# Attention and four experts on one core: where the last expert's first layer and its weight sums stand

## The chip, the cores and the metric

The kernel runs on one core of a Trainium2 chip. The metric is the device time of one execution in microseconds. A core has five engines, each with its own queue of instructions in order: TensorE (PE in the profile; PEld is its weight load), VectorE (DVE), ScalarE (ACT), GpSimd (POOL) and SyncE (SP, which here only issues DMAs). They wait for each other through semaphores. "Clock" is the TensorE clock that the throttle granted, as a share of full speed.

## The reference

Attention over 4 batches, 8 heads, 768 positions and head size 64; three heads see everything before them, five see 4 sink positions and a window of 64. Its output, as 3072 tokens of 512, goes through four experts that are summed with the tokens' weights.

```python
# attention
scores = scale * np.matmul(q, k.transpose(0, 1, 3, 2))
mask = np.where(retr[0, :, 0, 0, None, None], full_mask, stream_mask)
...
attn = np.matmul(a, v)                      # a: softmax of the masked scores
# experts: N, D = 3072, 512; E = 4, F = 1024
x = np.ascontiguousarray(attn_out.transpose(0, 2, 1, 3)).reshape(B * S, H * D)
p = domain_probs / (domain_probs.sum(-1, keepdims=True) + 1e-09)
for e in range(E):
    h = np.maximum(x @ w1[e], 0.0)
    out += p[:, e:e + 1] * (h @ w2[e])
```

## The kernel before

All matrices are held in f16. The 3072 tokens are 24 tiles of 128. The work has two strands. `attention(b, c)` makes the attention of half a batch (384 tokens, three tiles). `moe_steps()` makes the experts: tiles 0 to 2 together, then tile 3 alone ("the single tile"), both by `plain_steps`, and then ten pairs of tiles, 4-5 to 22-23, by `pair_steps`. Both strands are Python generators that yield after each step with the TensorE time that the step will take. The loop at the end of the kernel writes out the steps of the experts and, whenever the sum of the yielded times (weighted with a share) has passed a plan, the next step of attention. Instructions go into each engine's queue in this order, so the order of the whole program is fixed by hand. `require(g)` makes sure that an attention half is written out before something reads it.

**The single tile.** For each expert e: eight first-layer outputs (L983) with a Relu on ScalarE (L996), two half second layers (L1004) and an update of the output on VectorE (L1016, L1020). Behind experts 0 to 2 `last_weight_sum(e)` makes one VectorE subtraction for the second layer (L939, a helper, `minus`, that records all subtractions). Behind expert 1 the first pair's input for expert 0 is scaled. Behind expert 3 stand the four `first_weight_sums()`: the weights' sums and differences for expert 3's first layer, 128x1024 each. The fourth is made in place, in expert 3's own weights.

**A pair, first layer.** A token's weight is put on its input before the first layer (`scale_inputs`, L1066; the Relu lets a positive factor through). The inputs of experts 0 and 2 share one place in the buffer `xs`, expert 1 has its own, and expert 3 (EW) a third, with two more places for sums. Experts 0, 1 and 2 are plain: `plain_layer1(e)` has four steps of eight 256-column matmuls (L1100), each with one Relu (L1109). Expert 3 is done by a seven-product scheme of Strassen and Winograd (`winograd_layer1`): seven products of eight 128-column matmuls (L1152) in two PSUM buffers, x and y, with sums of its inputs before (`scaled_sums`: three small VectorE operations), copies of results (`keep`, ScalarE, L1162) and additions (`add`, VectorE, L1168 and L1174) between them. `keep(0)` writes a buffer "s1", `keep(1)` and `keep(2)` write "o1", which has the same memory (tag "o", one buffer) as the output tile `o` of the second layer. A product that goes on in the bank of an earlier one has to wait for the copy or the addition that reads it.

**A pair, second layer.** All four experts are one product of 4096 by 512, again in seven products (L1234), each in two halves, with sums of weights (`tsb`) and of activations (L939, L1074), copies (L1252, L1302) and additions (`add`, L1255). Behind the fifth product the next pair's input for expert 0 is scaled. Behind the sixth the first half of the output is stored, behind the seventh the second half (L1262, SP).

**Order in a pair's first layer.** `scale_inputs(nt0, 1)` comes first. The list `sums` is worked off, one entry behind each plain step. `load_probs(nxt)`, which loads the next pair's token weights through SP, stands ahead of expert 2.

**Queues around it.** SP issues the stores, the token weights and, for attention, the DMA transposes of keys, queries and results (L255, L718). GpSimd issues the loads of q, k and v. VectorE also masks attention's exponentials (L666), scales its results (L705 to L712, L779) and copies keys by windows and rows (L282, L286, L290, L266). ScalarE makes the exponentials (L662) and logarithms (L774, L784). The four "pA" banks are shared by plain steps and attention's scores.

Of the kernel before, what the change touches and what calls it, by code (L numbers as in the profile page):

```python
# [12 lines left out]
ALU = mybir.AluOpType  # L13
# [4 lines left out]
def kernel(  # L18
# [33 lines left out]
    nc = tc.nc  # L52
    P = 128
    B, H, S, D = q.shape
    E, DM, F = moe_w1.shape
# [43 lines left out]
    def bank():  # L99
        return pA.tile([P, 512], FP32, name="pA", bufs=4)  # L100
# [5 lines left out]
    HT = F // P // 2  # L106
# [4 lines left out]
    EW = E - 1  # L111
    KH, FN = DMP // 2, F // 2
# [19 lines left out]
    XS = 3 * DMP * 2 * P  # L132
# [247 lines left out]
    for h in range(H):  # L380
        if h == 2:
            nc.sync.dma_start(
                out=v_s32, in_=v[0, :, 0:NS, :].rearrange("h r d -> r h d")
# [16 lines left out]
        out=probs, in_=moe_domain_probs.rearrange("(t p) e -> p t e", p=P)  # L400
# [121 lines left out]
    def mm_ns(cols):  # L522
        return cols / 2.4 + 2.5
# [407 lines left out]
    def b_rows(k, n, e):  # L931
        f0 = e * FTP + k * HT
        return w2sb[:, f0 : f0 + HT, n * HN : (n + 1) * HN]
# [4 lines left out]
    def minus(out, a, b):  # L938
        nc.vector.tensor_tensor(out=out, in0=a, in1=b, op=ALU.subtract)  # L939
# [7 lines left out]
    def w1_part(j, k):  # L947
        return w1sb[:, EW * DMP + j * KH : EW * DMP + (j + 1) * KH, k * FN : (k + 1) * FN]

    def first_weight_sums():  # L950

        t = [t1sb[:, n, :, :] for n in range(3)]
        return [
            lambda: minus(t[0], w1_part(0, 1), w1_part(0, 0)),
            lambda: minus(t[1], w1_part(1, 1), t[0]),
            lambda: minus(t[2], w1_part(1, 0), t[1]),
            lambda: minus(w1_part(0, 1), w1_part(1, 1), w1_part(0, 1)),
        ]

    def last_weight_sum(e):  # L960

        minus(b_rows(0, 1, e), b_rows(1, 1, e), b_rows(0, 1, e))
# [68 lines left out]
    def pieces(nt0):  # L1031

        g0, j0 = divmod(nt0, 3)
        n0 = min(3 - j0, PT)
        yield g0, j0 * P, 0, n0
        if n0 < PT:
            yield g0 + 1, 0, n0, PT - n0

    pB_of = {}
    xs_of = [None]  # L1040

    def load_probs(nt0):
        pB_of[nt0] = moe.tile([P, PT, E, P], FP32, name="pB", tag="pB", bufs=1)
        rows = p_rows[nt0 : nt0 + PT, :]
        nc.sync.dma_start(
            out=pB_of[nt0].rearrange("p t e x -> p (t e x)"),
            in_=bass.AP(rows.tensor, rows.offset, [[0, P], [1, PT * E * P]]),
        )

    def scaled(e):  # L1050
        n = 2 if e == EW else e % 2
        x = xs_of[0][:, n * DMP * PC : (n + 1) * DMP * PC]
        return x.rearrange("p (c x) -> p c x", c=DMP)

    def scale_inputs(nt0, e):

        if xs_of[0] is None:
            xs_of[0] = moe.tile([P, XS + 2 * KH * P], FP16, name="xs", tag="xs", bufs=1)
        xs = scaled(e)
        for g, c0, t0, n in pieces(nt0):  # L1060
            require(g)
            xin = xT[g][:, :, c0 : c0 + n * P].rearrange("p c (t x) -> p c t x", t=n)
            o = xs[:, :, t0 * P : (t0 + n) * P].rearrange("p c (t x) -> p c t x", t=n)
            pb = pB_of[nt0][:, t0 : t0 + n, e, :]
            pb = pb.rearrange("p t (c x) -> p c t x", c=1)
            nc.vector.tensor_tensor(  # L1066
                out=o, in0=xin, in1=pb.to_broadcast([P, DMP, n, P]), op=ALU.mult
            )

    def input_sums(k0, k1):  # L1070
        k = slice(k0, k1)

        def s1():
            nc.vector.tensor_tensor(  # L1074
                out=S1[:, k, :], in0=A21[:, k, :], in1=A22[:, k, :], op=ALU.add
            )

        return [
            s1,
            lambda: minus(S3[:, k, :], A11[:, k, :], A21[:, k, :]),  # L1080
        ]
# [4 lines left out]
    def pair_steps(nt0, nxt):  # L1086

        sums = []

        def step_done():  # L1090
            if sums:
                sums.pop(0)()

        def plain_layer1(e):
            xs = scaled(e)
            for f0 in range(0, FTP, 2):
                ps = bank()
                for f in range(2):
                    for ct in range(DMP):
                        nc.tensor.matmul(  # L1100
                            out=ps[:, f * PC : (f + 1) * PC],
                            lhsT=w1sb[:, e * DMP + ct, (f0 + f) * P : (f0 + f + 1) * P],
                            rhs=xs[:, ct, :],
                            start=(ct == 0),
                            stop=(ct == DMP - 1),
                        )
                b0 = 2 * (f0 // HT)
                k0 = e * HT + f0 % HT
                nc.scalar.activation(  # L1109
                    out=blocks[:, b0 : b0 + 2, k0 : k0 + 2, :].rearrange(  # L1110
                        "p t f x -> p f t x"
                    ),
                    in_=ps.rearrange("p (f t x) -> p f t x", f=2, t=2),
                    func=AF.Relu,
                )
                step_done()
                yield 2 * DMP * mm_ns(PC), 0.5

        def x_part(i, j):
            return scaled(EW)[:, j * KH : (j + 1) * KH, i * P : (i + 1) * P]  # L1120

        def x_sum(n):
            x = xs_of[0][:, XS + n * KH * P : XS + (n + 1) * KH * P]
            return x.rearrange("p (c x) -> p c x", c=KH)

        def scaled_sums():
            def s1():
                nc.vector.tensor_tensor(
                    out=x_sum(0), in0=x_part(1, 0), in1=x_part(1, 1), op=ALU.add
                )  # L1130

            return [
                s1,
                lambda: minus(x_sum(1), x_sum(0), x_part(0, 0)),
                lambda: minus(x_part(1, 0), x_part(0, 0), x_part(1, 0)),
            ]

        def winograd_layer1():

# [64 lines left out]
            yield ns, 0.5  # L1204

        scale_inputs(nt0, 1)
        sums += [lambda: scale_inputs(nt0, EW)]
        if nt0 == pair0:
            sums += [lambda: last_weight_sum(E - 1)]
        sums += scaled_sums()  # L1210
        yield from plain_layer1(0)
        products = winograd_layer1()
        for e in (1, 2):
            if e == 1:
                scale_inputs(nt0, 2)
            elif nxt is not None:
                load_probs(nxt)
            for step in plain_layer1(e):
                yield step
                step = next(products, None)  # L1220
                if step is not None:
                    yield step
            sums += input_sums(0, 2 * HT) if e == 1 else input_sums(2 * HT, 4 * HT)
        for op in sums:
            op()

# [2 lines left out]
        x = pO.tile([P, DM], FP32, name="pO", bufs=2)[:, 0:HN]  # L1229
# [24 lines left out]
        def add(n, ps, i, j):  # L1254
            nc.vector.tensor_tensor(  # L1255
                out=o[:, i, j * HN : (j + 1) * HN], in0=ps, in1=s[:, n, :], op=ALU.add
            )

        def store(i, j=None):
            r = slice((nt0 + i) * P, (nt0 + i + 1) * P)  # L1260
            c = slice(0, DM) if j is None else slice(j * HN, (j + 1) * HN)
            nc.sync.dma_start(out=out[r, c], in_=o[:, i, c])  # L1262
# [31 lines left out]
        yield half  # L1294
        yield from product(y, S4, b(1, 1), False)
        add(1, y, 0, 1)
        store(0)
        if last:
            store(1, 1)
        yield half  # L1300
        yield from product(x, A22, t(2), False)
        nc.scalar.copy(out=o[:, 1, 0:HN], in_=x)  # L1302
        if last:
            store(1, 0)
        else:
            store(1)
        yield half

    pairs = list(range(pair0, NTILE, PT))

    def moe_steps():
        for e in range(E):
            if e == 1:
                turn_probs()
            yield from plain_steps(0, 3, e, lambda: xT[0], (e % 2) * FTP * CH)
            weight_sums(e)
        for e in range(E):
            n0 = (e % 2) * FTP * P
            yield from plain_steps(3, 1, e, lambda: xT[1][:, :, 0:P], n0)
            if e + 1 < E:  # L1320
                last_weight_sum(e)
            if e == E - 3:
                scale_inputs(pairs[0], 0)
        for op in first_weight_sums():
            op()
        for n, nt0 in enumerate(pairs):
            yield from pair_steps(nt0, pairs[n + 1] if n + 1 < len(pairs) else None)

# [55 lines left out]
    def require(a):  # L1384
        drained = False
        while state["a"] <= a:
            attention_step()
            drained = True
        if drained:
            tick(LAG)  # L1390
        while any(g <= a for _, _, g in behind):
            behind.pop(0)[1]()
# [48 lines left out]
```

The softmax here doesn't subtract the row's maximum and nothing guards it: scores larger than these inputs give would overflow.

## Time and profile before

| what | us |
|---|---|
| median of 5 runs | 386.87 (385.84 to 388.4) |
| the profiled execution, time | 386.8 |
| its span | 384.9 |
| TensorE busy | 373.2 (97%) |
| VectorE busy | 268.7 (70%) |
| ScalarE busy | 229.3 (60%) |
| GpSimd busy | 111.2 (29%) |
| mean granted clock of TensorE | 0.996 |

The shares are averages over stretches with different loads: up to about 90 us the kernel starts up, loads weights and works on tiles 0 to 3 beside attention. Then come the ten pairs, at 90.9, 125.9, 156.8, 185.4, 215.4, 244.4, 272.5, 302.7, 329.8 and 355.8 us (the first step's start of each), with attention beside the first eight. The last pair's second layer begins at 369.4 and TensorE ends before 382. In the timeline a row gives start, duration, engine, line, operation, output and input; in brackets stands the idle time of the engine before it and what ended it. Merged rows ("x2") give the time of all of them.

### The profile page before, as it was taken

What the parts mean: (1) busy time and instruction counts of PE and PEld (TensorE: products, weight loads), DVE (VectorE), ACT (ScalarE), POOL (GpSimd) and SP (SyncE); (2) the same over time, 40 slices, a digit from 0 to 9 for tenths busy, and PEclk for the clock granted to TensorE, in tenths of its full rate; (3) what the DMA queues carried; (4) which work ended last, traced back from release to release, by engine and by line L of the source; (5) the groups of instructions that cost most, each with busy time, mean ns of one, the idle gap of its engine ahead of it and who ended that gap; (6) DMA issues with size and microseconds to landing.
All of it is one profiled execution on the core that took longest, in us unless ns stands there. A gap on an engine that the chain in (4) does not pass through costs nothing.

```text
span 384.9 us, 9934 instructions
## 1 busy us (share of the span) xinstructions
PE 373.2 (97%) x4054; PEld 313.2 (81%) x4054; DVE 268.7 (70%) x590; ACT 229.3 (60%) x476; POOL 111.2 (29%) x152
## 2 busy tenths in 40 slices
PE   8999899998899999999999999999999999999996
PEld 4755456576798898899998988899998999998995
DVE  7746687567886878877766757977767867665460
ACT  3863568647486777665674775665665675450630
POOL 8933662953037217403710116403200000000000
PEclk9999999999899999999999999999999999999999
DMA  9999999999389989963990489964700210200001
GB/s 160 165 209 200 184 190 184 146 190 121 53 131 85 134 134 86 160 133 26 140 105 14 98 131 60 161 133 29 110 35 12 71 54 2 95 19 27 29 2 54
DMA packets 127193, 39.20 MB, mean 102 GB/s; under 512 B 116232, under 2 KB 120876, under 8 KB 127148
## 3 DMA queue, kind: packets, MB, share of 16 engines
q0 software_dynamic: 86816, 19.01, 56.5%
q1 hardware_dynamic: 38732, 19.18, 21.9%
q8 instruction: 31, 0.51, 0.5%
q10 hardware_dynamic: 1600, 0.39, 0.5%
q14 instruction: 14, 0.11, 0.1%
HBM read 44.88 MB, written 6.34 MB: 133 GB/s over the span
## 4 chain that ended last, share of the span: by engine, by line
PE 76%; DMA 11%; DVE 4%; POOL 4%; SPq 2%; ACT 2%; issue 1%; POOLq 0%; ACTq 0%
PE pO L1234 32%; PE pA L1100 24%; PE pO L1152 7%; DMA w2sb<-in_moe_w_dram 7%; PE pA L644 4%; PE pO L1004 2%; PE pA L983 2%; DMA qT<-q 2%; PE pV L692 2%; SPq L255 2%; PE pV L756 2%; DMA vR<-in_v_dram 1%; POOL vS L302 1%; DMA out_dram<-o 1%; POOL vR L296 1%
## 5 line engine op out<-in xcount | busy, mean ns | idle before, releaser
L1100 PE MATMUL pA<-xs,w1sb 128*128 128x256 f16 x960 | 120.9, 274 | 3.0 <-DVE xs L1066 3.0
L1234 PEld LDWEIGHTS <-hA 128*128 128x128 f16 x1120 | 106.5, 98 | 13.3 <-issue 0.5
L1100 PEld LDWEIGHTS <-w1sb 128*128 128x128 f16 x960 | 90.2, 98 | 13.2 <-DVE xs L1066 3.6
L1109 ACT ACTIVATE hA<-pA 128x512 f16<-128x512 f32 x120 | 71.1, 597 | 42.0 <-PE pA L1100 39.9
L662 ACT ACTIVATE es<-pA 128x384 f16<-128x384 f32 (+2 forms) x122 | 59.1, 511 | 32.7 <-PE pA L644 28.5
L1234 PE MATMUL pO<-w2sb,hA 128*128 128x256 f16 x640 | 78.1, 272 | 0.4 <-DVE hA L1168 0.4
L298 POOL DMA_DIRECT2D vS<-in_v_dram x30 | 29.6, 989 | 128.6 <-PE pV L756 121.2
L1234 PE MATMUL pO<-tsb,hA 128*128 128x256 f16 x480 | 58.9, 272 | 0.0
L1066 DVE TENSOR_TENSOR xs<-xT,pB 128x1024 f16<-128x1024 f16 (+1 forms) x52 | 48.7, 970 | 4.2 <-PE pA L1100 4.2
L939 DVE TENSOR_TENSOR hA<-hA 128x1024 f16<-128x1024 f16 x60 | 39.6, 685 | 0.6
L996 ACT ACTIVATE hA<-pA 128x384 f16<-128x384 f32 (+1 forms) x64 | 22.3, 386 | 20.3 <-PE pA L983 17.8
L983 PE MATMUL pA<-xT,w1sb 128*128 128x384 f16 (+1 forms) x256 | 31.7, 273 | 0.1
L1004 PE MATMUL pO<-w2sb,hA 128*128 128x512 f16 x128 | 30.5, 379 | 0.8 <-DMA w2sb<-in_moe_w_dram 0.8
L779 DVE TENSOR_TENSOR xT<-pV,rc 64x384 f16<-64x384 f32 x37 | 20.5, 555 | 11.8 <-ACT rc L784 9.6
L774 ACT ACTIVATE rc<-pV,eps 64x384 f32<-64x384 f32 x37 | 21.3, 575 | 9.1 <-PE pV L756 8.5
L983 PEld LDWEIGHTS <-w1sb 128*128 128x128 f16 x256 | 19.3, 98 | 8.4 <-issue 0.5
L666 DVE TENSOR_TENSOR es<-es,mS 128x384 f16<-128x384 f16 (+1 forms) x40 | 13.6, 345 | 16.8 <-ACT es L662 16.6
L1152 PE MATMUL pO<-xs,w1sb 128*128 128x128 f16 x320 | 25.1, 223 | 0.0
L644 PE MATMUL pA<-qT,kR 128*128 128x384 f16 (+2 forms) x120 | 22.9, 278 | 0.6 <-ACT qT L555 0.4
L1255 DVE TENSOR_TENSOR o<-pO,s 128x256 f32<-128x256 f32 x30 | 12.7, 422 | 14.9 <-PE pO L1234 11.8
L1074 DVE TENSOR_TENSOR hA<-hA 128x1024 f16<-128x1024 f16 x20 | 13.8, 688 | 12.7 <-ACT hA L1109 12.5
L1004 PEld LDWEIGHTS <-hA 128*128 128x128 f16 x128 | 11.9, 98 | 12.8 <-issue 1.0
(130 smaller groups left out, 468.8 us busy)
## 6 DMA issues: line engine op xcount, KB each, us to landing
pB<-p_rows SPq DMA_DIRECT2D x10, 512.0 KB, 3.4
out_dram<-o SPq DMA_DIRECT2D x19, 256.0 KB, 4.3
w1sb<-in_moe_w_dram POOLq DMA_DIRECT2D x8, 512.0 KB, 9.9
w2sb<-in_moe_w_dram POOLq DMA_DIRECT2D x4, 1024.0 KB, 13.2
vS<-in_v_dram POOLq DMA_DIRECT2D x30, 112.0 KB, 3.5
k_rows<-in_k_dram POOLq DMA_DIRECT2D x18, 128.0 KB, 4.2
q<-in_q_dram POOLq DMA_DIRECT2D x18, 128.0 KB, 5.5
vR<-in_v_dram POOLq DMA_DIRECT2D x24, 48.0 KB, 5.1
```

What stands on the lines that cost most here:

```text
L298: gp.dma_start(out=t[:, :, own_v(h)], in_=windows_of(v, b, h, c))
L644: nc.tensor.matmul(out=ps[:, o : o + nq], lhsT=key_tile(b, c, h, t), rhs=qTs[b, c][:, hp, q0 : q0 + nq], start=(n == 0 or not first), stop ...
L662: nc.scalar.activation(out=es[:, 0:cols], in_=ps[:, 0:cols], func=AF.Exp, scale=SC)
L939: nc.vector.tensor_tensor(out=out, in0=a, in1=b, op=ALU.subtract)
L983: nc.tensor.matmul(out=pss[ft][:, 0:cols_n], lhsT=w1sb[:, e * DMP + ct, ft * P : (ft + 1) * P], rhs=x[:, ct, :], start=(n == 0), stop=(n = ...
L996: nc.scalar.activation(out=hs[:, ft, :], in_=ps[:, 0:cols_n], func=AF.Relu)
L1004: nc.tensor.matmul(out=ps_o, lhsT=hs[:, ft, j * P : (j + 1) * P], rhs=w2sb[:, e * FTP + ft, :], start=(ft == 0), stop=(ft == FTP - 1),)
L1066: nc.vector.tensor_tensor(out=o, in0=xin, in1=pb.to_broadcast([P, DMP, n, P]), op=ALU.mult)
L1100: nc.tensor.matmul(out=ps[:, f * PC : (f + 1) * PC], lhsT=w1sb[:, e * DMP + ct, (f0 + f) * P : (f0 + f + 1) * P], rhs=xs[:, ct, :], start= ...
L1109: nc.scalar.activation(out=blocks[:, b0 : b0 + 2, k0 : k0 + 2, :].rearrange("p t f x -> p f t x"), in_=ps.rearrange("p (f t x) -> p f t x" ...
L1152: nc.tensor.matmul(out=ps[:, f * P : (f + 1) * P], lhsT=w[:, ct, f * P : (f + 1) * P], rhs=a[:, ct, :], start=(first and f == 0 and ct == ...
L1234: nc.tensor.matmul(out=ps, lhsT=a[:, k, :], rhs=b(k), start=(first and k == 0), stop=(k == KT - 1), skip_group_check=not first,)
```

## The change

The three small functions `x_part`, `x_sum` and `scaled_sums` leave `pair_steps` and stand beside it, and `scaled_sums` now does its three operations at once. Three of the four first-layer weight sums are made behind the single tile's experts 0, 1 and 2; the fourth goes to the first step of the first pair. The first pair's inputs for experts 0 and 3 are scaled behind experts 1 and 2 of the single tile, and its input sums are made behind expert 3. In the other pairs, expert 3's input is scaled behind the sixth product of the second layer of the pair before, and its sums are made behind the seventh. In the first layer the seven products follow the third plain step of expert 0 and each of the next six steps, up to the first step of expert 2; before, they followed the four steps of expert 1 and the first three of expert 2.

```diff
+    def scaled_sums():
+        nc.vector.tensor_tensor(
+            out=x_sum(0), in0=x_part(1, 0), in1=x_part(1, 1), op=ALU.add
+        )
+        minus(x_sum(1), x_sum(0), x_part(0, 0))
+        minus(x_part(1, 0), x_part(0, 0), x_part(1, 0))
...
         scale_inputs(nt0, 1)
-        sums += [lambda: scale_inputs(nt0, EW)]
         if nt0 == pair0:
-            sums += [lambda: last_weight_sum(E - 1)]
-        sums += scaled_sums()
-        yield from plain_layer1(0)
+            sums += [first_weight_sums()[3], lambda: last_weight_sum(E - 1)]
         products = winograd_layer1()
-        for e in (1, 2):
+        n = 0
+        for e in range(E - 1):
             if e == 1:
                 scale_inputs(nt0, 2)
-            elif nxt is not None:
+            elif e == 2 and nxt is not None:
                 load_probs(nxt)
             for step in plain_layer1(e):
                 yield step
-                step = next(products, None)
+                step = next(products, None) if n > 1 else None
+                n += 1
                 if step is not None:
                     yield step
-            sums += input_sums(0, 2 * HT) if e == 1 else input_sums(2 * HT, 4 * HT)
+            if e:
+                sums += input_sums(0, 2 * HT) if e == 1 else input_sums(2 * HT, 4 * HT)
...
         yield from product(y, S4, b(1, 1), False)
         add(1, y, 0, 1)
+        if nxt is not None:
+            scale_inputs(nxt, EW)
         store(0)
...
         yield from product(x, A22, t(2), False)
         nc.scalar.copy(out=o[:, 1, 0:HN], in_=x)
+        if nxt is not None:
+            scaled_sums()
...
             if e + 1 < E:
                 last_weight_sum(e)
-            if e == E - 3:
-                scale_inputs(pairs[0], 0)
-        for op in first_weight_sums():
-            op()
+            if e + 1 < E:
+                first_weight_sums()[e]()
+            if e > 0:
+                (
+                    lambda: scale_inputs(pairs[0], 0),
+                    lambda: scale_inputs(pairs[0], EW),
+                    scaled_sums,
+                )[e - 1]()
```

## The prediction

> **What bounds the kernel now.** I read the page first (parts 1 and 2), then who waited for whom on TensorE, then the timeline where a wait stands, then busy time in short stretches. TensorE is busy 97% of the span, and in the last pair, which has no attention beside it, the chain runs without a hole. So only two things can move the end: waits of TensorE, and its clock. The list of its waits:
>
> ```profile
> PE pA L1100 <- DVE xs L1066: 3.0, 2, 2.8
> PE pO L417 <- DVE early L402: 1.3, 1, 1.3
> ...
> PE pO L1234 <- DVE hA L1168: 0.4, 1, 0.4
> ```
>
> One wait of 2.8 us for a scaled input stands out. The timeline puts it at the start of the first pair (rows of VectorE and TensorE; a row in brackets ends with the idle time before it):
>
> ```profile
> 93.86 0.69 DVE L939 TENSOR_TENSOR t1sb<-w1sb 128x1024 f16<-128x1024 f16 x1
> 94.58 1.42 DVE L939 TENSOR_TENSOR t1sb<-w1sb,t1sb 128x1024 f16<-128x1024 f16 x2
> 95.91 0.69 DVE L939 TENSOR_TENSOR w1sb<-w1sb 128x1024 f16<-128x1024 f16 x1
> 96.51 2.35 DVE L1066 TENSOR_TENSOR xs<-xT,pB 128x1024 f16<-128x1024 f16 x2
> 97.78 1.05 PE L1100 MATMUL pA<-xs,w1sb 128*128 128x256 f16 x8 [2.76 <-DVE xs L1066]
> ```
>
> VectorE does the four first-layer weight sums and only then scales the input of expert 1, for which TensorE has been waiting since 95.02. There is a second cost behind it, seen in the stretches (length, busy PE, PEld, DVE, ACT, POOL, then granted clock):
>
> ```profile
> 17.14:20.55 3.41, 2.08 (x26) 1.59 (x24) 1.80 (x5) 2.01 (x5) 1.85 (x5) 1.00 1.40 194
> 95.65:99.06 3.41, 1.27 (x17) 1.19 (x18) 3.38 (x6) 0.14 (x2) 0.00 (x0) 1.00 0.00 1
> 99.90:100.90 1.00, 1.00 (x7) 0.67 (x6) 1.00 (x6) 0.54 (x1) 0.00 (x0) 0.50 0.09 20
> 102.50:104.00 1.50, 1.50 (x25) 1.41 (x24) 1.43 (x5) 0.53 (x2) 0.00 (x0) 1.00 0.56 112
> ```
>
> Finer stretches put the fall at 99.06 and the return at 102.47: 3.41 us at clock 0.50, which cost a busy TensorE 1.70 us. So the first pair loses 2.76 + 1.70 = 4.46 us, and that is all there is to win, but for a wait of 0.37 us at 230.42 and one of 0.26 at 160.86.
>
> **The change, part by part.** I write P0, P1, P2 for the steps of experts 0 to 2 (0.87 us each on TensorE by the chain) and W1 to W7 for the products of expert 3 (0.45 us each: one started at 222.75, the step behind it at 223.20). Before: four P0, then P1 W1 P1 W2 P1 W3 P1 W4 P2 W5 P2 W6 P2 W7 P2. After: P0 P0 P0 W1 P0 W2, P1 W3 P1 W4 P1 W5 P1 W6, P2 W7 P2 P2 P2. TensorE, ScalarE and VectorE do the same instructions, none added or removed; no DMA is added. Attention is drawn in by the sum of TensorE time given out; that sum is the same at the start of every second layer, so there attention stands where it stood.
>
> *Single tile.* Three sums (0.69 each) and the scaling of expert 3 (1.22, row 84.25) move here. VectorE's idle time in the timeline is 2.17 us before 82.98, 0.23 before 86.49, 1.06 before 89.10 and 1.21 before 90.53. Behind expert 0 the sum fits. Behind expert 1 the scaling of expert 0 and then the key copies (L266, 85.38) come 0.69 later; TensorE loads the first copied keys at 86.46, and the first copy would end at about 86.55: wait 0.15, bounds 0 and 0.7. Behind expert 2 come 0.69 + 1.2; with the lateness of 0.46 left, 2.35 us stand against gaps of 2.27, so at 90.95 VectorE is where it was, within 0.1. Were these gaps not there, the head masks and the window copies (L282, to 93.73; TensorE uses them at 93.81) would be late next.
>
> *First pair.* From 93.86 VectorE does three sums of 0.28 (row 100.19), not 2.65 us of weight sums: expert 1 is scaled by 95.87, not 97.68. TensorE asks for it after W1 and W2, at 95.02 + 0.90 = 95.92: nothing to 0.1 is left, and with the wait the clock's fall goes. Next comes W4, which writes the bank that the sum behind W2 (L1168, 0.69) reads. Ahead of that sum VectorE now has the fourth weight sum 0.60, the head's scaling 0.67, the second-layer weight sum 0.60 and masks 0.41, so it ends near 98.8; TensorE is there at 95.95 + 0.87 + 0.45 + 0.87 + 0.34 of attention = 98.5. Wait 0.3, bounds 0 and 0.8. First pair: -4.46 + 0.15 + 0.05 + 0.30 = -3.96.
>
> *Later pairs, VectorE.* Scaling expert 3 (1.2) and its sums (0.84) go ahead of the scaling of expert 1, that is 2.04 us more there, against 0.90 us by which W1 and W2 put off its use, and VectorE's idle time. Where attention copies its key windows just then, this is too much. Third pair: before, the scaling ended at 160.76 and TensorE waited 0.26; after, add at 154.55, 1.2, masks, 2.23 of copies, 0.84, 0.68 and the scaling itself end at 161.8 against a use at 161.5: 0.4, so 0.15 more. Sixth pair (scaling at 246.25, hardly an idle moment before it): end at 249.4 against 249.1: 0.35. Bounds for the two together: 0, and 2 x (2.04 - 0.90) = 2.3 if none of VectorE's idle time helps. In the others the scaling ends 1 us or more ahead. W1 itself needs expert 3's input 2.6 us into the pair, and it is there.
>
> *The output tile.* W3's copy writes a buffer that the store of the pair before must have left. Between fourth and fifth pair that store is late, because SP issues six transposes first:
>
> ```profile
> 213.47 0.33 SPq L1262 DMA_DIRECT2D out_dram<-o  x1
> 213.86 3.85 SPq L255 DMA_TRANSPOSE kT<-k_rows  x3
> 217.80 3.83 SPq L255 DMA_TRANSPOSE qT<-q  x3
> 221.73 0.53 SPq L1262 DMA_DIRECT2D out_dram<-o  x1
> ...
> 225.11 0.58 ACT L1162 COPY o<-pO 128x512 f32<-128x512 f32 x1 [1.57 <-DMA out_dram<-o]
> ...
> 225.75 0.61 PE L1152 MATMUL pO<-xs,w1sb 128*128 128x128 f16 x8
> ```
>
> W5 adds into the bank that this copy reads, and before it started 0.06 us after the copy's end: just in time. After, W5 stands behind three P1 and four W, so TensorE reaches it at 224.25 - 0.87 + 0.45 = 223.82 on the same scale, and the store lands no sooner: wait 1.93. Bounds: 1.0, if the store or attention shifts by a step, and 2.1, if the 0.18 of attention falls behind W5. ScalarE's outputs behind the copy wait too, but four banks cover them. The wait of 0.37 at 230.42 goes, as the last product ends two steps sooner. In the other pairs the store lands in time: the closest is the last, 356.29 + 4.9 (the longest landing) = 361.2 against a copy at 361.6.
>
> *The clock there.* Does a wait of 1.93 us make it fall? The trace shows a stretch of 3.41 us with 2.14 us idle that did, and one with 1.33 us idle (17.14) that did not. Where the stretches lie against the wait is not fixed; over all positions the fuller one holds 1.66 us of it on average (1.93 in 43% of them, down to 0.97), which is nearer 1.33 than 2.14. I take 0; bounds 0 and 1.70.
>
> The Trainium skill ("TensorE: Matmul & The Clock Gate", section "Why this matters for your kernels") says that gaps over some 3 us between bursts drop the clock, with one window of idle as the reason. The row of 95.65 differs: 2.76 us of waiting was enough. By the rule the 1.93 us would be safe and the sum stays as it is; by the row it may cost 1.70.
>
> **Sum.** -3.96 + 0.15 + 0.35 + 1.93 - 0.37 = -1.90 us. The profiled execution took 386.8 us (span 384.9, the rest lies around it), so 384.9. The median of the runs shown is 386.87, that is 0.07 above, so 385.0.
>
> **Rivals.**
> 1. *The clock falls in the fifth pair*, in most executions: 385.0 + 1.7 = 386.7. For it: a whole wait in one stretch leaves 1.48 us busy, close to the 1.27 that fell. Against: it must lie whole. A chance of 0.25.
> 2. *The store's wait doesn't reach TensorE*: without 1.93 the time is 383.1. For it: landing took 3.3 us of a queue that can change. Against: SP's order is written out, and the row of 225.75 shows no slack. 0.08.
> 3. *The first wait is only moved* (slower). The sums and the scaling are put between experts 0 to 2, and VectorE there has 4.7 us idle by the rows above, but only 2.5 of it behind expert 1. If its work there doesn't fit, the key copies, the window copies and the scaling of expert 1 are all late at one place, 86 to 96. From about 1.7 us of lateness at 90.95 on the wait is back near 1.7 us with the two small ones, the clock falls as now, the first pair gains under 0.5, and the 2.06 of the other places decide: 386.87 - 0.5 + 2.06 = 388.4. Against: the gaps were counted. 0.15 with everything of this sign.
> 4. *No change*: expert 1's input still sets the first pair, but in part: about 386.5. 0.05.
>
> **How the numbers follow.** The forecast, at 0.47, is 385.0, its own range 384.0 to 385.7 by the small bounds. A run of this kernel is told from no change at 0.3%, 1.16 us: faster means under 385.7, slower over 388.0. Faster: 0.47 + 0.08 = 0.55. Same: rivals 1 and 4, 0.25 + 0.05 = 0.30. Slower 0.15. The range reaches to rival 2 below and past rival 1 above, with 0.9 us for VectorE's waits: 383.0 to 387.6; rival 3 stays out.
>
> **What would show it.** The wait of 2.76 at the first P1 gone or under 0.3 and clock 1.00 from 90 to 110; the scaling of expert 1 ending near 95.9; a wait of TensorE at W5 of the fifth pair near 1.9 us, with a ScalarE copy that waited over 3 us for the store; waits of some 0.4 us on L1066's scaling in the third and sixth pairs, none at the start of the fifth pair's second layer. I am wrong if the first pair still waits over 1 us, if the clock falls elsewhere, or if W5 does not wait.

## The result and the profile after

| | before | after |
|---|---|---|
| median, us | 386.9 (51 runs) | 385.13 (30 runs) |
| ratio, 95% interval | | 0.9959 (0.9946 to 0.9971) |
| profiled execution: time, span, us | 386.8, 384.9 | 384.4, 382.7 |
| mean granted clock in it | 0.996 | 1.000 |

The forecast was 385.0 (range 383.0 to 387.6). The change is a gain of 0.41% (0.29 to 0.54). The list of TensorE's waits after, from the first pair on (engine, line, what it waited for, us in total, times, longest):

```profile
PE pO L1147 <- ACT o L1157: 1.7, 1, 1.7
PE pO L1147 <- DVE hA L1163: 1.0, 1, 1.0
PE pA L1114 <- DVE xs L1066: 0.2, 1, 0.2
```

The large wait for expert 1's scaled input is gone and two others have come (L1147 is a product of expert 3, L1163 the sum behind one, L1157 the copy). The timeline at the first pair:

```profile
94.60 1.22 DVE L1066 TENSOR_TENSOR xs<-xT,pB 128x1024 f16<-128x1024 f16 x1
...
95.43 0.61 PE L1147 MATMUL pO<-xs,w1sb 128*128 128x128 f16 x8
...
95.88 1.05 PE L1114 MATMUL pA<-xs,w1sb 128*128 128x256 f16 x8
...
98.01 0.15 DVE L705 TENSOR_SCALAR rs<-pV 128x3 f32<-128x3 f32 x1
...
98.69 0.68 DVE L1163 TENSOR_TENSOR hA<-pO,s 128x512 f16<-128x512 f32 x1
...
99.42 0.61 PE L1147 MATMUL pO<-xs,t1sb 128*128 128x128 f16 x8 [0.99 <-DVE hA L1163]
```

Expert 1's input is ready at 95.82 and its first step starts at 95.88, straight behind W2 (95.43): no wait. But W4 waits 0.99 us for the sum behind W2, ahead of which VectorE did a second head's scaling (98.01). The stretches show that the clock does not fall (length, busy PE, PEld, DVE, ACT, POOL, then clock, DMA share and GB/s):

```profile
90.00:100.00 10.00, 9.01 (x118) 7.86 (x117) 9.28 (x28) 6.90 (x14) 1.92 (x3) 1.00 1.11 107
100.00:110.00 10.00, 10.00 (x133) 9.18 (x130) 8.29 (x18) 7.88 (x15) 2.00 (x2) 1.00 0.76 99
```

The fifth pair, where the store comes late, and the third:

```profile
158.38 1.05 PE L1114 MATMUL pA<-xs,w1sb 128*128 128x256 f16 x8 [0.22 <-DVE xs L1066]
...
219.02 0.53 SPq L1257 DMA_DIRECT2D out_dram<-o  x1
...
221.52 0.59 ACT L1157 COPY o<-pO 128x512 f32<-128x512 f32 x1 [3.27 <-DMA out_dram<-o]
...
222.16 0.61 PE L1147 MATMUL pO<-xs,w1sb 128*128 128x128 f16 x8 [1.72 <-ACT o L1157]
```

ScalarE stood 3.27 us before the copy (1.57 before the change), and now TensorE stands behind it for 1.72.

Where the time went, by the start of the steps in the two traces (first step of a first layer to the first of its second layer):

| first layer of pair | before, us | after, us | difference |
|---|---|---|---|
| first | 19.62 | 16.15 | -3.47 |
| third | 15.05 | 15.01 | -0.04 |
| fifth | 15.07 | 16.28 | +1.21 |
| sixth | 14.62 | 14.71 | +0.09 |

All other stretches agree to 0.02 us. The sum, -2.21, agrees with the difference of the spans (384.9 and 382.7).

### The profile page after: what moved, and what is told of

The parts are those of the page before. It is cut to its first block, busy times and chain, and to the rows that moved or that the text cites. A ratio compares the mean times of both kernels' runs of the same rounds, so it can differ in the third digit from the quotient of the medians.

```text
span 382.7 us, 9934 instructions
## 1 busy us (share of the span) xinstructions
PE 370.7 (97%) x4054; PEld 311.8 (81%) x4054; DVE 268.5 (70%) x590; ACT 230.1 (60%) x476; POOL 111.7 (29%) x152
## 4 chain that ended last, share of the span: by engine, by line
PE 79%; DMA 7%; DVE 5%; POOL 3%; SPq 2%; ACT 1%; issue 1%; POOLq 0%; ACTq 0%
PE pO L1229 31%; PE pA L1114 24%; PE pO L1147 7%; DMA w2sb<-in_moe_w_dram 7%; PE pO L1004 5%; PE pA L983 4%; PE pA L644 4%; SPq L255 2%; PE pV L756 2%; PE pV L692 2%; DVE xs L1066 1%; DVE kS L282 1%; POOL vS L302 1%; ACT es L662 1%; DMA out_dram<-o 1%
## 5 line engine op out<-in xcount | busy, mean ns | idle before, releaser
L1114 PE MATMUL pA<-xs,w1sb 128*128 128x256 f16 x960 | 119.0, 273 | 0.2 <-DVE xs L1066 0.2
L1114 PEld LDWEIGHTS <-w1sb 128*128 128x128 f16 x960 | 89.8, 98 | 9.7 <-DVE xs L1066 0.4
L939 DVE TENSOR_TENSOR hA<-hA 128x1024 f16<-128x1024 f16 x60 | 39.7, 686 | 0.8
L983 PEld LDWEIGHTS <-w1sb 128*128 128x128 f16 x256 | 19.3, 98 | 8.4 <-issue 0.5
L1147 PE MATMUL pO<-xs,w1sb 128*128 128x128 f16 x320 | 24.4, 219 | 1.7 <-ACT o L1157 1.7
L1147 PEld LDWEIGHTS <-w1sb 128*128 128x128 f16 x320 | 20.6, 98 | 2.6 <-issue 1.8
```

The lines of the kernel that those rows point to most:

```text
L983: nc.tensor.matmul(out=pss[ft][:, 0:cols_n], lhsT=w1sb[:, e * DMP + ct, ft * P : (ft + 1) * P], rhs=x[:, ct, :], start=(n == 0), stop=(n = ...
L1114: nc.tensor.matmul(out=ps[:, f * PC : (f + 1) * PC], lhsT=w1sb[:, e * DMP + ct, (f0 + f) * P : (f0 + f + 1) * P], rhs=xs[:, ct, :], start= ...
L1147: nc.tensor.matmul(out=ps[:, f * P : (f + 1) * P], lhsT=w[:, ct, f * P : (f + 1) * P], rhs=a[:, ct, :], start=(first and f == 0 and ct == ...
```

## The experiments

Each kernel is timed beside the kernel before, and the recorded ratio to it stands with its interval. There were three sets. In the first, with the first four kernels, the kernel before had a median of 387.17 us; in the second, with "The products at their old place" and the first timing of "Two weight sums later in the first pair", 387.56; in the third, with both second timings and the waits of a chosen length, 386.49. The recorded ratios differ by up to 0.002 from the quotients of the medians, so medians of different sets are compared only roughly. The clock of each execution was also recorded, and it matters below.

**The weight sums alone.** The kernel before, with products and scaling where they were:

```diff
@@ moe_steps, single tile
+            if e + 1 < E:
+                first_weight_sums()[e]()
             if e == E - 3:
                 scale_inputs(pairs[0], 0)
-        for op in first_weight_sums():
-            op()
@@ pair_steps
         sums += scaled_sums()
+        if nt0 == pair0:
+            sums += [first_weight_sums()[3]]
```

> The kernel before, with only the weight sums moved: three behind the single tile's experts 0 to 2, the fourth at the end of the first pair's list. Theory (the wait for expert 1's scaled input and the clock's fall behind it are the gain, 4.46 us): VectorE scales expert 1 at once, done near 95.0 us, so the first P1 waits under 0.3 us and the clock stays 1.00 from 90 to 110 us; expert 3's input comes about 0.3 late for W1, and W4 waits about 1.3 us for the sum behind W2, because VectorE stays the slower engine there. No wait for the store in the fifth pair, since W5 stands where it stood. Time 386.9 - 4.46 + 1.6 = 384.0. Rival (the gain comes from the products' new place and from scaling expert 3 sooner): 386.5 or more, with the first P1 still waiting over 1 us.

384.14 us, 0.9943 (0.9922 to 0.9965). Its waits from the first pair on:

```profile
PE pO L1152 <- DVE hA L1168: 0.9, 1, 0.9
PE pO L1236 <- DVE hA L1168: 0.4, 1, 0.4
PE pA L1100 <- DVE xs L1066: 0.3, 1, 0.3
```

No wait for expert 1's input in the first pair (the 0.3 is the old one of the third pair), clock 1.00 from 90 to 110, and 0.9 at W4. The theory holds; the rival, 386.5 or more, falls. This part alone gives the whole gain. Its median is 1 us below that of the full change, but the intervals of the two ratios overlap and the spans of the two profiled executions agree (382.6 and 382.7), so that it is better is not shown.

**The idle time filled.** The kernel before, with matmuls that do nothing useful in the wait:

```diff
@@ pair_steps, ahead of expert 1's first step
+        if nt0 == pair0:
+            ps = bank()
+            for _ in range(11):
+                nc.tensor.matmul(
+                    out=ps, lhsT=ident16, rhs=w1sb[:, 0, 0:512], start=True, stop=True
+                )
```

> The kernel before, with eleven 512-column matmuls whose result is not used, put ahead of the first pair's first P1, so that TensorE is busy for some 2.4 us of its 2.76 us wait. The wait for the scaled input itself stays. Theory: the clock falls because of that idle time, so it stays 1.00 from 90 to 110 us, and 1.70 us of slow matmuls are gone; but with a fast TensorE W4 comes before the sum behind W2 is done on VectorE (103.8 us) and waits about 0.75. Time 386.9 - 0.95 = 385.9. Rival 1: the fall costs its full 1.70, 385.2, and W4 doesn't wait. Rival 2: VectorE sets the whole stretch and the clock costs nothing, 386.9.

385.66 us, 0.9979 (0.9958 to 0.9999). The rows of the timeline and two stretches of it:

```profile
97.53 1.05 PE L1100 MATMUL pA<-xs,w1sb 128*128 128x256 f16 x8 [0.39 <-DVE xs L1066]
...
103.61 0.61 PE L1152 MATMUL pO<-xs,t1sb 128*128 128x128 f16 x8 [0.29 <-DVE hA L1168]
```

```profile
90.00:100.00 10.00, 9.61 (x93) 7.20 (x92) 9.55 (x23) 5.34 (x11) 0.53 (x1) 1.00 0.67 67
100.00:110.00 10.00, 9.71 (x136) 8.98 (x134) 8.49 (x25) 7.70 (x14) 1.03 (x1) 1.00 0.67 102
```

The step still starts where it did (97.53 against 97.78), but the clock stays up, and by the ratio the time falls by 0.8 us (by the medians of this set 1.5). Of its 12 executions 2 have a mean clock of 0.9965 or less, of the 25 of the kernel before beside it 19: the fall came from TensorE's idle time. Both rivals fall, though narrowly: the interval of the ratio leaves out 385.2 (0.9956) and 386.9 (1.0), and W4 does wait, which rival 1 had ruled out (0.29 in the profiled execution, less than the expected 0.75).

The gain was not the full 1.70, because of that wait and because not every execution of the kernel before has the fall. Of 59 of them whose clock was recorded, 40 have a mean clock of 0.9965 or less, and a fall of 3.41 us to 0.50 is 0.0044 of the mean; ten have 0.991 or less, as two falls give. Of the changed kernel's 31 (its profiled one among them), 7 have 0.9965 or less. Only a trace tells where a fall stands. Between executions with a fall and the others the medians differ by 1.1 to 1.8 us (387.51 and 385.74 in the set of this experiment). The average of the mean clocks is 0.9957 before and 0.9986 after; over a span of 385 us that is about 1.1 us, as a mean over executions, of a gain whose medians differ by 1.77.

**The weight sums put back.** The changed kernel, with three of the four sums behind expert 3 again:

```diff
-            if e + 1 < E:
-                first_weight_sums()[e]()
...
+        for op in first_weight_sums()[:3]:
+            op()
```

> The changed kernel with three of the four weight sums put back behind the single tile's expert 3 (one part undone). Theory: the scaling of expert 1 ends 2.05 us later, near 97.9, and the first P1 (asked for at 95.9) waits about 2.0 us; W4 waits about 1 us as before. If the clock doesn't fall on a wait of 2.0 us: 385.1 + 2.0 = 387.1. If it falls, 0.7 to 1.7 more: 387.8 to 388.8. Rival (the place of the sums doesn't matter): 385.1.

387.5 us, 1.0014 (0.9993 to 1.0034): the whole gain is gone. The waits, and the stretches of the first and the fifth pair:

```profile
PE pO L1147 <- ACT o L1157: 2.3, 1, 2.3
PE pA L1114 <- DVE xs L1066: 2.0, 2, 1.8
PE pO L1147 <- DVE hA L1163: 1.0, 1, 1.0
```

```profile
90.00:100.00 10.00, 8.18 (x103) 6.98 (x101) 9.10 (x25) 5.78 (x12) 0.00 (x0) 1.00 0.57 61
100.00:110.00 10.00, 9.01 (x114) 8.16 (x113) 8.23 (x21) 7.48 (x14) 1.03 (x1) 1.00 0.77 102
220.00:230.00 10.00, 7.67 (x99) 7.02 (x97) 4.87 (x11) 6.04 (x12) 0.98 (x1) 1.00 0.90 124
```

A first wait of 1.8 us and a store wait of 2.3, and the clock fell behind neither. That is the first branch of the expectation, but for the store's wait, which grew by 0.6 us; the expectation did not have that, and why it grew stays open.

**The copies in other memory.** The changed kernel; S1 is written behind the first step of expert 2 at the earliest, in VectorE's queue behind the two additions that read the copies:

```diff
-            o = moe.tile([P, PT, DM], FP32, name="o1", tag="o", bufs=1)
+            o = hA[:, 4 * KT * P :].bitcast(FP32).rearrange("p (n x) -> p n x", n=PT)
```

> The changed kernel with the two product copies (keep 1 and keep 2) in the part of the activations' memory that holds S1, which is free at that time, and not in the output tile's memory. Theory: no copy waits for a store, W5 of the fifth pair doesn't wait, and 1.72 us are gone: 385.1 - 1.7 = 383.4, ratio to before 0.991. The wait of about 1 us at W4 of the first pair stays. Rival (the store's wait covers another one, of ScalarE or attention, that then takes its place): 385.1, with a wait of over 1 us within 3 us of W5 in the fifth pair.

383.51 us, 0.9923 (0.9899 to 0.9948). The second timing was to compare it with the next kernel:

> The kernel with the copies in S1's memory, a second time, so that it and the next kernel are timed on one chip. Theory: ratio to before 0.991 to 0.993.

383.04 us, 0.991 (0.9884 to 0.9937). All the waits that are left from the first pair on, in the second profile:

```profile
PE pO L1147 <- DVE hA L1163: 0.9, 1, 0.9
PE pA L1114 <- DVE xs L1066: 0.2, 1, 0.2
```

No wait for a store on ScalarE or TensorE, and nothing in its place. The rival, another wait behind it, falls.

**Two weight sums later in the first pair.** On top of the last kernel:

```diff
-        if nt0 == pair0:
-            sums += [first_weight_sums()[3], lambda: last_weight_sum(E - 1)]
...
             if e == 1:
+                if nt0 == pair0:
+                    first_weight_sums()[3]()
                 scale_inputs(nt0, 2)
             elif e == 2 and nxt is not None:
+                if nt0 == pair0:
+                    sums += [lambda: last_weight_sum(E - 1)]
                 load_probs(nxt)
```

> The kernel with the copies in S1's memory, and in the first pair the fourth first-layer weight sum and the last second-layer weight sum moved behind the sum that follows W2 (they stood ahead of it, 0.60 us each on VectorE). Theory (W4 of the first pair waits for that sum, which is late by the work ahead of it): it ends near 98.1 and not 99.4 us, the wait of 0.93 us at W4 is under 0.2, and some 0.2 may come back at W5 or W6: 383.5 - 0.75 = 382.8. Rival (VectorE sets the whole stretch, so the wait only moves on to W5, W6 or expert 2's input): 383.5, with waits that again sum to 0.9 us between 97 and 104 us.

381.73 us, 0.986 (0.9832 to 0.9889), better than expected by 1 us, which called for the second timing:

> The kernel that also moves two weight sums behind the sum that follows W2, a second time beside the one without. By the traces the first pair's first layer is 1.09 us shorter (14.99 against 16.08), so the ratio to before should be 0.003 below that of the other kernel, 0.988 to 0.990. If the first timing's difference of 0.006 comes again, something outside the first pair differs too.

381.82 us, 0.9866 (0.984 to 0.9891). In one set, the two kernels differ by 1.2 us in the median, against 1.09 by the traces, so scatter of six runs can account for the surplus of the first timing. That is not settled: the two ratios differ by 0.0044 where 0.003 was expected, and 0.9866 lies below the expected 0.988 to 0.990, which is inside its interval. The waits from the first pair on, in the second profile:

```profile
PE pA L1114 <- DVE xs L1066: 0.2, 1, 0.2
```

The sum behind W2 now starts at 97.55, not 98.69, and W4 waits for nothing: the wait did not move on, so the rival falls. This is the best version: 1.3% faster than the kernel before and about 0.9% faster than the changed one.

**The products at their old place.** The changed kernel with one number changed:

```diff
-                step = next(products, None) if n > 1 else None
+                step = next(products, None) if n > 3 else None
```

> The changed kernel with the seven products back at their old place (behind the four steps of expert 1 and three of expert 2); the weight sums and expert 3's scaling stay moved. Theory (the sooner products gave the scaling of expert 1 0.9 us, and cost the wait for the store): the wait at W5 of the fifth pair (1.72) goes and the old 0.37 at its second layer comes back; the first pair waits 0.8 for expert 1's input but no longer 1.0 at W4; the third pair waits 1.1 and the sixth 0.8 for the same input. Sum: -1.72 + 0.37 + 0.8 - 1.0 + 0.9 + 0.8 = +0.15, 385.3. Rival 1 (the products' sooner place is a gain): 386.5 or more. Rival 2 (it is the change's only cost): 383.8, with no waits for expert 1's input.

386.08 us, 0.9968 (0.9947 to 0.9989). Its waits for expert 1's input stand in the first, third and sixth pair:

```profile
98.88 1.05 PE L1114 MATMUL pA<-xs,w1sb 128*128 128x256 f16 x8 [0.84 <-DVE xs L1066]
...
161.30 1.05 PE L1114 MATMUL pA<-xs,w1sb 128*128 128x256 f16 x8 [1.30 <-DVE xs L1066]
...
230.88 1.03 PE L1229 MATMUL pO<-w2sb,hA 128*128 128x256 f16 x8 [0.37 <-DVE hA L1163]
...
249.65 1.05 PE L1114 MATMUL pA<-xs,w1sb 128*128 128x256 f16 x8 [0.82 <-DVE xs L1066]
```

They are 0.84, 1.30 and 0.82, where 0.8, 1.1 and 0.8 were expected, and the old 0.37 is back. By steps' starts the first layers of these pairs and the fifth differ from the changed kernel's by 0.64 us in all, not 0.15. The theory's mechanism holds with a size somewhat off. Both rivals (386.5 or more; 383.8 with no such waits) miss.

**Waits of a chosen length.** The kernel with both moves, with work put ahead of expert 1's scaling in the two last pairs: six additions (short) or eight (long).

```diff
+        for _ in range({20: 6, 22: 6}.get(nt0, 0)):
+            nc.vector.tensor_tensor(
+                out=kSf[:, 0:1024], in0=kSf[:, 1024:2048], in1=kSf[:, 2048:3072],
+                op=ALU.add,
+            )
         scale_inputs(nt0, 1)
```

> The kernel with both moves, and in the last two pairs, which have no attention, six VectorE additions (128x1024, into key memory that is no longer read) ahead of the scaling of expert 1: TensorE waits about 1.7 us in each. Theory (the clock falls when a stretch of 3.41 us, whose place is not fixed, holds enough idle time, between 1.33 and 2.14 us of it): a fall in fewer than 4 of 10 such waits, the time 3.3 us above the kernel without the additions, and up to 1 us more by falls. Rival 1 (only waits of some 3 us count): none. Rival 2 (any wait above 1.4 us): a fall in nearly every one, and the time 3.3 + 3.4 above.

> The same with eight additions: TensorE waits about 2.9 us in each of the last two pairs. Theory: a fall in 7 to 8 of 10 such waits, so most executions have one or two, each 1.7 us and 0.0044 of the mean granted clock; the time 5.7 + 2.5 us above the kernel without the additions. Rival 1 (only waits over 3.4 us count): no fall, 5.7 above. Rival 2 (every such wait): 5.7 + 3.4 above, two falls in each execution.

Short: 385.72 us (0.9976, 0.996 to 0.9993), 3.9 us above the kernel with both moves, with waits of 1.88 and 1.74 us in the profiled execution, and a mean clock of 0.999 or 1.000 in each of twelve executions: no fall in 24 waits. Long: 392.56 us (1.0143, 1.0119 to 1.0168), 10.7 us above, with waits of 3.34 and 3.20, which are longer than expected, and a mean clock of 0.991 (two falls) or 0.987 (three) in each of six executions. The trace, one with three, has one fall behind each of the two waits and one at 21.5 us; that the other five also have two behind these waits is taken from their mean clock. A stretch at the wait and the one behind it, first short, then long:

```profile
330.00:335.00 5.00, 3.44 (x40) 3.19 (x41) 3.80 (x8) 2.11 (x4) 0.00 (x0) 1.00 0.05 18
335.00:340.00 5.00, 5.00 (x60) 4.62 (x58) 3.27 (x6) 2.92 (x6) 0.00 (x0) 1.00 0.24 90
```

```profile
330.00:335.00 5.00, 1.66 (x20) 1.38 (x19) 4.84 (x8) 1.04 (x2) 0.00 (x0) 1.00 0.00 0
335.00:340.00 5.00, 5.00 (x44) 4.28 (x42) 1.70 (x4) 2.56 (x5) 0.00 (x0) 0.66 0.32 105
```

The theory's branch for short waits holds (fewer than 4 of 10, and it was none), and the rival that any wait over 1.4 us costs the clock falls. For the long ones all fell, as rival 2 of that expectation had it, where the theory had 7 to 8 of 10; twelve of twelve is unlikely by such a share, but not excluded. The rival that only waits over 3.4 us count falls too, if narrowly (3.20).

## Why the prediction was right

| step | predicted, us | the trace after |
|---|---|---|
| first wait and the clock behind it | -2.76 - 1.70 | gone, clock 1.00 |
| key copies behind expert 1 of the single tile | +0.15 | 0 |
| rest of the first wait | +0.05 | 0 |
| W4 of the first pair | +0.30 (0 to 0.8) | +0.99 |
| third pair | +0.15 | -0.04 |
| sixth pair | +0.35 | +0.09 by starts, no wait |
| W5 of the fifth pair, for the store | +1.93 | +1.72 |
| second layer of the fifth pair | -0.37 | gone |
| clock behind the store's wait | 0 (bound 1.70) | 0 |

**The bound.** TensorE's waits and its clock set the end, and their list accounts for the difference of the two traces. That the weight sums are what mattered is shown twice, by moving them alone (384.14) and by putting them back (387.5).

**The moved work in the single tile.** It fits into VectorE's gaps, as counted. The two key copies took 0.51 us and not 0.88 and were done at 86.42, when TensorE came at 86.47.

**The one term outside its bounds is W4.** "Wait 0.3, bounds 0 and 0.8" was 0.99. Attention's next step, the second head's values and their scaling (0.67 on VectorE), was written out ahead of the sum behind W2, where I had put it behind. Its TensorE part stands at 95.25, just ahead of W2 at 95.43, so it came early by a single step, and nothing in the bounds allowed for it: the sum ended at 99.37 and not near 98.8, and TensorE, with less attention ahead of W4, was there at 98.26 and not at 98.5. That the wait is made of the work ahead of the sum is shown by the kernel that takes 1.2 us of it away and waits for nothing.

**Two scales.** The profile's idle time counts from a matmul group's modelled end, which lies 0.16 or 0.17 us behind the place where the next step starts when nothing holds it up (a plain step is shown with 1.04 where steps follow each other by 0.87, a product with 0.61 where they follow by 0.45). Some terms of the prediction go by one scale and some by the other. By the steps' starts W4 waited 1.16 (99.42 - 97.39 - 0.87) and W5 1.89 (222.16 - 220.09 - 0.18).

**Third and sixth pair.** In the third the foreseen wait is there: by the steps' starts 0.38 (158.38 - 157.55 - 0.45), where 0.4 was foreseen. It is no longer than before, 0.43 on the same scale (160.86 - 159.56 - 0.87); the prediction had compared its 0.4 with the profile's 0.26 and so came to 0.15 more. In the sixth TensorE asked when foreseen, 4.67 us behind the layer's start (246.76 - 242.09), but the input was ready after 4.70 (246.79) and not after the foreseen 4.98 (249.4 - 244.42). The window copies up to 243.99 had taken 2.18 us where they took 2.32 before, and the three sums 0.73 where the prediction had 0.84. So P1 started 0.09 late, where 0.35 was foreseen. That the late input can hold TensorE up is shown with the products at their old place (waits of 1.30 and 0.82).

**The store.** The copy waits for the store, and the product for the copy; with another memory both are gone, and the fifth pair's first layer is 1.91 us shorter in the traces (14.37 against 16.28; by the ratios to the kernel before the whole gains 1.4 and 1.9 us). By the steps' starts the forecast of 1.93 was right to 0.04.

**The clock.** To take 0 was right: the wait's 1.72 us of idle time lay whole in one stretch of 3.41 (219.94 to 223.36, by the last section), the case that rival 1 needed, and the clock stayed; waits of 1.74 and 1.88 us never cost it in 24 cases. No run has just 1.93. The Trainium skill ("TensorE: Matmul & The Clock Gate", "Why this matters for your kernels") warns of gaps over some 3 us; against one row I had held that 2.76 was enough. Both have a part: 3.20 us and more cost the clock in all twelve cases, and in the kernel before, whose wait is 2.76, 40 of 59 executions show a fall. What the prediction left out is that not every execution of the kernel before pays the 1.70: as a mean the clock's part of the gain is some 1.1 us. The median hid that, as most executions have a fall.

The errors have both signs (by the table 0.69 too little at W4; 0.15, 0.05, 0.19, 0.26 and 0.21 too much elsewhere), so the sum of -1.90 against -2.21 in the traces and -1.77 in the medians is in part good luck.

## What to carry to other kernels

Where TensorE is busy nearly all the time, list its waits and read the granted clock behind each: a wait of 2.76 us cost up to 4.5. Work that must come before a start goes into gaps of the engine that does it, counted one by one; here three operations of 0.69 us moved gave all of the gain. When steps are pulled forward, look at the buffer that they write, not only at what they read: the sooner products met a store that had been just in time, and using memory that was free at that moment gave that wait back, 1.4 and 1.9 us by the two timings.

## What the runs showed of the hardware

- The clock does not depend on the length of a wait alone. It fell behind a wait of 2.01 us at 41.26 in the profiled execution of the kernel with the products at their old place (a wait for weights at the start), and not behind one of 2.33 us in the fifth pair of the kernel with the sums put back. The clock records of the traces show what makes the difference. Each of the six falls in them ahead of TensorE's end starts a whole number of stretches of 3.413 us behind the first clock record of its trace (27 in the kernel before, 11 with the products at their old place, 5 in the first trace with both moves, 5, 97 and 106 with the long waits). This raster lies elsewhere in each execution: the first record stands at 4.5 to 7.3 us. Cut along it, the stretch straight ahead of each fall holds 2.01 to 2.45 us without TensorE work, and none of the other 1306 stretches of the twelve traces, up to TensorE's end, holds more than 1.88. The wait of 2.33 us lay across a boundary, 1.41 in one stretch and 0.91 in the next. The stretches at the wait of 2.01 and, with the sums put back, at the wait of 2.33:

```profile
38.97:42.38 3.41, 1.40 (x12) 0.51 (x12) 0.60 (x1) 0.84 (x3) 1.81 (x4) 1.00 1.20 132
```

```profile
220.63:224.05 3.42, 2.01 (x28) 1.78 (x27) 1.15 (x2) 0.00 (x0) 0.00 (x0) 1.00 1.33 151
224.05:227.46 3.41, 2.50 (x37) 2.35 (x37) 0.66 (x2) 3.11 (x7) 0.12 (x1) 1.00 0.46 154
```

- So no wait of up to 1.88 us cost the clock in these traces, and whether a longer one did went by where it lay. An estimate from these numbers: with a place left to chance, a wait of 2.76 us puts 1.88 to 2.01 us into one stretch in 0.63 to 0.71 of the cases. It fits the 40 of 59 executions of the kernel before, some of which have their fall elsewhere.
- Each fall seen in a trace lasts 3.41 us at half clock. After the change 24 of 31 executions have a mean clock above 0.9965. Where the others have their fall was not recorded; three of the other profiled executions have one in the first 50 us (from 22.4, 42.4 and 21.5 us on), the first behind a wait of 2.25 us for values, the second behind the one of 2.01 us for weights.
